# Cosformer attention and a quick-gelu layer on one core: v copied ahead of q's evictions, and three moves in the opening

## The chip, the cores and the metric

The kernel runs on one core of one Trainium2 chip. The metric is the device time of an execution in microseconds. A core has five engines that run side by side and wait for each other through semaphores: PE (TensorE, matrix products, with its weight loads shown as PEld), DVE (VectorE), ACT (ScalarE), POOL (GpSimd) and SP (SyncE). Here POOL and SP issue the transfers between the chip's main memory and the core. PE writes its results into eight banks of an accumulation memory (PSUM), and DVE or ACT carry them from there into the working memory, which the texts call an eviction.

## The reference

Eight batches, eight heads, 576 positions, head size 64, all in float32. The first half is a linear attention with positions weighted by a cosine and a sine; the second half is a layer of 512 to 2048 to 512 with g = h * sigmoid(1.702 h).

```python
def phi(x, c, s):
    r = np.maximum(x, 0.0)
    return np.concatenate([r * c, r * s], axis=-1)
q_p, k_p = phi(q, cos_w, sin_w), phi(k, cos_w, sin_w)
kv = np.einsum('bhsf,bhsd->bhfd', k_p, v)
z = np.sum(k_p, axis=2)
num = np.einsum('bhsf,bhfd->bhsd', q_p, kv)
den = np.einsum('bhsf,bhf->bhs', q_p, z)[..., None] + 1e-06
x = (num / den).transpose(0, 2, 1, 3).reshape(B * S, H * D)
h = x @ w_in
out = (h * (1.0 / (1.0 + np.exp(-1.702 * h)))) @ w_out
```

## The kernel before, in words

The work goes batch by batch. For one batch, q and k are made positive and weighted by the cosine and the sine (`trig`, line 143 on DVE and POOL, line 141 on ACT). The key-value sums `kv_mm` (line 228) multiply the weighted k with v, 72 small matmuls for four pairs of heads. The weighted q is turned so that features lie on partitions. For batches 0 and 1 PE does that with transposes: `qturn_pe` (line 184) fills a PSUM tile with two of the nine slots of 64 positions, and `qevac` evicts it to `qT` on DVE (line 202) or on ACT (line 200). `num_mm` (line 258) makes numerators and denominators of a chunk of 128 positions, `num_div` (lines 264, 266, 308) divides on DVE, `xturn_mm` (line 328) turns the quotient on PE and `xturn_evac` (line 334) evicts it to `xT` on ACT. Then the layer: `mm1` (line 349) makes h for 16 groups of 128 hidden features, `gelu` (line 354, ACT) makes g of each, and `mm2` (line 386) multiplies by w_out for four chunks of 128 rows, in portions of four hidden groups each. Output goes through ACT (line 390) and a transfer that POOL issues (line 394).

Nothing reorders the work: each engine runs its instructions in the order in which the program writes them, and waits come from data and from buffers. So the order of the calls is the schedule. Buffers are few. The eight PSUM banks are four banks m0 to m3, taken in the order 2, 0, 3, 1 or named by `at`, and two tiles of two banks each that `pair` gives in turn. `at_homes` takes such a pair as the home of two `qturn_pe`. In block 0, `ha` holds slots 0 to 3 of batch 1, `hb` slots 4 to 7, and the next pair, which `kv_open` takes for batch 1's key-value sums, is the one that `ha` had: `kv_mm` can't start until both evictions of `ha` are done. Likewise `hc`, for the ninth slot, is the one that `hb` had.

The opening, batch 0, is written out by hand in lines 410 to 490, with its own small steps. `idle` (line 400) gives PE 512-column matmuls on zeros: three in float32 at the start, and one at line 424 and one at line 436, in bfloat16. v of batch 0 comes in bfloat16 straight from memory (`vb`, line 133, in two halves). `den_early` (line 273) and `num1_mm` (line 284) make denominators and numerators of chunks 0 and 1, `num1_div` (line 289) divides, `x1turn_mm` (line 296) turns and `x1turn_evac` (line 300) evicts to `xT`. Slots 6 and 7 of q go one by one through `qslot_pe` (line 189) and `qslot_evac` (line 193), slot 8 through `qturn_pe(4, at=1)`. The first four hidden groups are made chunk by chunk with `part(c, fc)`, matmuls of 128 columns, and the group that follows (`mm1(0, 4)`) takes the bank that the first gelu frees.

Block 0 (lines 500 to 558) is the layer of batch 0 with the attention of batch 1 among its matmuls. k, q and v of batch 1 come in float32 by transfers from POOL's queue (line 116), between the four parts of w_out. `vcopy` brings v of batch 1 into the bfloat16 tile `vt`, for two pairs of heads at a time (line 164 on DVE, line 162 on ACT). From batch 1 on, blocks look alike: `mm1` and `gelu` for 16 groups, then `mm2` with the next batch's key-value sums and numerators between, and q turned by transfers.

Of the kernel before, what the change touches and what calls it, by code (L numbers as in the profile page):

```python
# [19 lines left out]
def kernel(  # L20
# [97 lines left out]
    def load_q(b, eng=nc.sync):  # L118
        eng.dma_start(out=qf[:, 0:2048].rearrange("p (h e) -> p h e", h=H),
                            in_=q[b, :, 0:512, :].rearrange("h (p c) d -> p h (c d)", c=4))  # L120
        eng.dma_start(out=qf[0:64, 2048:2560].rearrange("p (h e) -> p h e", h=H),
                            in_=q[b, :, 512:S, :].rearrange("h p d -> p h d"))

    def load_win(g):
        nc.gpsimd.dma_start(out=w_in_sb[g], in_=win_r[:, :, ts(g, 512)])
# [10 lines left out]
    def trig(dst, src, j, act=False, eng=nc.vector):  # L136
        i = src[:, :, ts(j, 64)]
        for cs, w in enumerate((cosw, sinw)):
            o = dst[:, j, :, ts(cs, 64)]
            if act:  # L140
                nc.scalar.activation(o, i, AF.Relu, scale=w[:, j:j + 1])  # L141
            else:
                eng.tensor_scalar(o, i, 0.0, w[:, j:j + 1], op0=MAX, op1=MUL)  # L143
# [14 lines left out]
    def vcopy(i0, i1, act=False):  # L158
        o = vt[:, :, i0:i1, 0:64].rearrange("p j i e -> p i j e")
        i = vf[:, i0:i1].rearrange("p i (j e) -> p i j e", e=64)  # L160
        if act:
            nc.scalar.activation(o, i, AF.Copy)
        else:
            nc.vector.tensor_copy(o, i)
# [3 lines left out]
    def bank(shape, dt=F32, at=None):  # L168
        if at is None:
            at = (2, 0, 3, 1)[ring["m"] % 4]  # L170
            ring["m"] += 1
        return pmm.tile(shape, dt, name="mm", tag=f"m{at}", bufs=1)
# [7 lines left out]
    def qturn_pe(c, home=None, at=None):  # L180
        tps[c] = bank([128, 2, NI, 128], BF16, at) if home is None else home
        for j in range(2 * c, min(2 * c + 2, NS)):
            for i in range(NI):
                nc.tensor.transpose(tps[c][:, j % 2, i], qn0[:, j, i, :], ident)  # L184
# [10 lines left out]
    def qevac(c, act=False):  # L195
        n = min(2 * c + 2, NS) - 2 * c
        o = qT[:, :, ds(c * 128, n * 64)].rearrange("f h (j p) -> f j h p", j=n)
        i = tps.pop(c)[:, 0:n].rearrange("f j i (hh p) -> f j (i hh) p", hh=2)
        if act:
            nc.scalar.activation(o, i, AF.Copy)  # L200
        else:
            nc.vector.tensor_copy(o, i)  # L202
# [51 lines left out]
    def num_mm(c):  # L254
        ps = pair()
        for h in range(H):
            i, hh = divmod(h, 2)
            nc.tensor.matmul(ps[:, h // 4, ds((h % 4) * 65, 65)], qT[:, h, ts(c, 128)],  # L258
                             st["kvs"][:, hh, i, 0:65], start=True, stop=True)
        nums[c] = [ps]  # L260

    def inv_of(d):
        den = small.tile([128, 2, 4], F32, name="den")
        nc.vector.tensor_scalar(den, d, 1e-6, None, op0=ADD)  # L264
        inv = small.tile([128, 2, 4], F32, name="inv")
        nc.vector.reciprocal(inv, den)
        return inv
# [25 lines left out]
    def x1turn_mm(c):  # L293
        xv = nums.pop(c).rearrange("p a h e -> p (a h e)")
        for kc in range(KC):
            nc.tensor.transpose(st["n", c][:, ts(kc, 64)].bitcast(BF16), xv[:, ts(kc, 128)], ident)  # L296

    def x1turn_evac(b, c):
        i = st["n", c][:, 0:256].bitcast(BF16).rearrange("p (k t) -> p k t", k=KC)
        nc.scalar.activation(x_of(b, c), i, AF.Copy)  # L300

    def num_div(c, inv=None):
        ps = nums[c][0]
        pv = ps[:, :, 0:260].rearrange("p a (h e) -> p a h e", h=4)
        if inv is None:
            inv = inv_of(pv[:, :, :, 64])
        xn = small.tile([128, 2, 4, 64], BF16, name="xn", bufs=4)
        nc.vector.tensor_tensor(xn, pv[:, :, :, 0:64],  # L308
                                inv.unsqueeze(3).to_broadcast([128, 2, 4, 64]), op=MUL)
        nums[c].append(xn)  # L310
# [6 lines left out]
    def x_open(b):  # L317
        x[b] = xpool.tile([128, KC, MT], BF16, name="xT")
# [11 lines left out]
    def xturn_evac(b, c):  # L330
        ps = nums.pop(c)[0]
        i = ps[:, :, 264:392].bitcast(BF16).rearrange("p a (k t) -> p a k t", k=2)
        o = x_of(b, c).rearrange("p (a k) t -> p a k t", a=2)
        nc.scalar.activation(o, i, AF.Copy)

    def xturn_dma(b, c):
        xn = nums.pop(c)[1]
        n = 128 if c < 4 else 64
        nc.sync.dma_start_transpose(out=x_of(b, c), in_=xn[0:n].rearrange("p a h e -> p (a h e)"))
# [5 lines left out]
    def mm1_part(b, fc, t0, t1):  # L345
        if t0 == 0:
            hp[fc] = bank([128, MT])
        for kc in range(KC):
            nc.tensor.matmul(hp[fc][:, t0:t1], w_in_of(kc, fc), x[b][:, kc, t0:t1],  # L349
                             start=(kc == 0), stop=(kc == KC - 1))  # L350
# [30 lines left out]
    def mm2(b, t, lo, hi, c0=0, c1=d_model):  # L381
        if lo == 0:
            yp[t, c0] = bank([128, d_model])
        for fc in range(lo, hi):
            w = gT[fc][:, ts(t, 128)] if t < 4 else gl_t[:, fc, ts(t - 4, 128)]
            nc.tensor.matmul(yp[t, c0][:, c0:c1], w, w_out_sb[:, fc, c0:c1],  # L386
                             start=(fc == 0), stop=(fc == FC - 1))
        if hi == FC:
            ysb = ypool.tile([128, d_model], F32, name="ysb")
            nc.scalar.activation(ysb[:, c0:c1], yp[t, c0][:, c0:c1], AF.Identity)  # L390
            for p0, n, dst in rows(b, t):
                last = b == B - 1 and t != 4 and (t, p0) != (5, 0)
                eng = nc.sync if last else nc.gpsimd
                eng.dma_start(out=dst[:, c0:c1], in_=ysb[p0:p0 + n, c0:c1])  # L394

    def idle(n, w=None, t=warm):
        if w is None:
            w = bank([128, 512], at=0)
        for _ in range(n):
            nc.tensor.matmul(w, t[:, 0:128], t[:, 0:128].unsqueeze(1).to_broadcast([128, 4, 128]),  # L400
                             start=True, stop=True)
        return w
# [7 lines left out]
    w = idle(3, t=warm32)  # L410
# [10 lines left out]
        ksum(j, j == order[0], j == order[-1])  # L421
    for j in (0, 1):
        trig(qn0, qf0, j)
    idle(1, w)
    qturn_pe(0, at=2)
    for j in (2, 3):
        trig(qn0, qf0, j, act=True)
# [5 lines left out]
    nc.gpsimd.tensor_copy(gate[0:1, 1:2], vb[0:1, 3, 0:1])  # L433
    load_win(2)
    load_win(3)
    idle(1, w)
    qturn_pe(1, at=3)
    kv_mm(0, 2, vb_rhs, 0, 64)
    for j in (6, 7):
# [18 lines left out]
    qslot_evac(7)  # L458
    num_mm(2)
    num_div(2)  # L460
    x_open(0)
    x1turn_mm(0)
    x1turn_evac(0, 0)
    qturn_pe(4, at=1)
    num_mm(3)
    num_div(3)
    x1turn_mm(1)
# [3 lines left out]
    def part(c, *fcs):  # L471
        for fc in fcs:
            mm1_part(0, fc, c * 128, c * 128 + 128)
# [6 lines left out]
    part(1, 3)  # L480
    xturn_mm(3)
    xturn_evac(0, 3)
    part(2, 0, 1, 2, 3)
    num_mm(4)
    num_div(4)
    xturn_dma(0, 4)
    part(3, 0, 1, 2, 3)
    for fc in range(4):
        gelu(fc)
    mm1(0, 4)  # L490
# [22 lines left out]
    ha = at_homes()  # L513
    qturn_pe(0, ha[0])
    qturn_pe(1, ha[1])
    qevac(0)
    qevac(1, act=True)
    vcopy(0, 2)
    vcopy(2, 4)
    mm2(0, 3, 4, 8)  # L520
    hb = at_homes()
    qturn_pe(2, hb[0])
    qturn_pe(3, hb[1])
    qevac(2, act=True)
    qevac(3, act=True)
    load_q(2, nc.gpsimd)
    load(kf, k, 2, nc.gpsimd)
    load(vf, v, 2, nc.gpsimd)
# [109 lines left out]
```

## Time and profile before

| | |
|---|---|
| median of 3 runs | 291.74 us (291.6 to 292.91) |
| the profiled execution | 291.65 us |
| its span, first to last instruction | 289.9 us |
| instructions | 5634 |
| granted clock of PE, mean | 0.999 |
| opening, up to the first 512-column matmul of the layer | 20.39 us |
| block 0's last matmul gives way to block 1 | 50.59 us |

A row of the chain of work gives start, length and the work that the end of the program goes back to; "issue" is time in which nothing that the profile shows was waited for. A row of a timeline gives start, length, engine, line, operation, what is written and read, and in brackets the idle time of the engine ahead of it and what ended it. Consecutive instructions of one kind stand in one row with their count; its length runs from the first's start to the last's end. A matmul's length holds its passage through the array, so one of 512 columns shows 0.38 us while the next starts 0.216 us after it; pieces of the chain join such ends. A row of a tile or a line gives the least, median and greatest duration in ns, and for transfers the time from issue to landing.

### The profile page before, as it was taken

How to read it: one execution, taken by the hardware profiler on the slowest of the kernel's cores; microseconds unless marked ns; L12 is line 12 of the kernel's file. 1: busy time of each engine (PE TensorE's matmuls, PEld its weight loads, DVE VectorE, ACT ScalarE, POOL GpSimd, SP SyncE). 2: the span in 40 equal slices, each digit the busy share in tenths (PEclk: the TensorE clock that was granted, in tenths of full speed). 3: DMA queues.
4: the chain of work that ended last, by engine and by line, in shares of the span. 5: the costliest groups of instructions: out<-in, count | busy, mean ns of one | idle time of the engine just before them, and what ended most of it. 6: DMA issues, size and time to landing. Idle time of an engine off the chain costs nothing.

```text
span 289.9 us, 5634 instructions
## 1 busy us (share of the span) xinstructions
PE 285.1 (98%) x2253; PEld 152.8 (53%) x2253; DVE 122.9 (42%) x353; ACT 134.0 (46%) x235; POOL 37.7 (13%) x72
## 2 busy tenths in 40 slices
PE   8999999999999999999999999999999999999995
PEld 3685475555555545555455545554555455554444
DVE  4853566903657364636482567256534200000000
ACT  7977565692157114630463136412651167651111
POOL 6560043201210011001100110011000100002000
PEclk9999999999999999999999999999999999999999
DMA  7999999991999868956896469946962400002322
GB/s 254 240 215 286 372 257 371 233 234 34 134 296 247 192 139 298 260 171 144 256 296 184 129 188 321 232 103 180 324 125 73 119 37 0 0 2 46 85 86 72
DMA packets 67769, 52.46 MB, mean 181 GB/s; under 512 B 47968, under 2 KB 57952, under 8 KB 67744
## 3 DMA queue, kind: packets, MB, share of 16 engines
q1 hardware_dynamic: 60320, 32.52, 44.9%
q0 software_dynamic: 7424, 19.60, 23.9%
q8 instruction: 17, 0.28, 0.4%
q14 instruction: 8, 0.07, 0.1%
HBM read 36.70 MB, written 9.44 MB: 159 GB/s over the span
## 4 chain that ended last, share of the span: by engine, by line
PE 95%; DMA 2%; ACT 2%; DVE 1%; issue 0%; SPq 0%; ACTq 0%; DVEq 0%
PE mm L386 43%; PE mm L349 38%; PE mm L366 5%; PE at L228 3%; PE at L258 3%; DMA kf<-in_k_dram 2%; ACT kr L141 1%; PE mm L184 1%; PE at L328 0%; PE at L184 0%; ACT qT L200 0%; DVE qT L202 0%; DVE xn L289 0%; PE mm L296 0%; ACT xT L300 0%
## 5 line engine op out<-in xcount | busy, mean ns | idle before, releaser
L386 PE MATMUL mm<-w_out_sb,g 128*128 128x512 bf16 (+1 forms) x528 | 118.2, 373 | 0.0
L349 PE MATMUL mm<-xT,w_in 128*128 128x512 bf16 (+1 forms) x560 | 112.7, 361 | 0.1
L354 ACT ACTIVATE g<-mm 128x512 bf16<-128x512 f32 x128 | 75.6, 598 | 31.3 <-PE mm L349 31.3
L349 PEld LDWEIGHTS <-w_in 128*128 128x128 bf16 x560 | 60.0, 113 | 51.2 <-issue 0.2
L386 PEld LDWEIGHTS <-g 128*128 128x128 bf16 x528 | 48.6, 98 | 49.1
L390 ACT ACTIVATE ysb<-mm 128x512 f32<-128x512 f32 (+1 forms) x37 | 21.7, 586 | 105.9 <-PE mm L386 103.0
L394 POOL DMA_DIRECT2D out_dram<-ysb x39 | 21.1, 542 | 205.0 <-ACT ysb L390 204.6
L143 DVE TENSOR_SCALAR kr<-kf,cosw 128x256 bf16<-128x256 f32 x64 | 22.4, 350 | 29.9 <-DMA kf<-in_k_dram 29.9
L308 DVE TENSOR_TENSOR xn<-at,inv 128x512 bf16<-128x512 f32 x38 | 26.3, 691 | 1.3
L143 DVE TENSOR_SCALAR kr<-kf,sinw 128x256 bf16<-128x256 f32 x64 | 22.5, 352 | 0.0
L264 DVE TENSOR_SCALAR den<-at 128x8 f32<-128x8 f32 x38 | 6.3, 166 | 32.9 <-PE at L258 32.9
L233 DVE CAST kvs<-at 128x520 bf16<-128x520 f32 (+1 forms) x9 | 5.8, 640 | 32.9 <-PE at L228 32.9
L258 PEld LDWEIGHTS <-qT 128*128 128x128 bf16 x304 | 14.1, 97 | 8.0
L258 PE MATMUL at<-kvs,qT 128*128 128x65 bf16 x304 | 15.4, 193 | 0.0
L156 DVE TENSOR_SCALAR qn<-qf,sinw 128x512 bf16<-128x512 f32 (+1 forms) x30 | 14.4, 480 | 0.0
L156 DVE TENSOR_SCALAR qn<-qf,cosw 128x512 bf16<-128x512 f32 (+1 forms) x30 | 14.3, 476 | 0.0
L366 PE MATMUL mm<-xt,w_in 128*128 128x512 bf16 x64 | 14.0, 379 | 0.0
L386 PE MATMUL mm<-w_out_sb,gl_t 128*128 128x512 bf16 x64 | 14.0, 379 | 0.0
L367 ACT ACTIVATE gl_t<-mm 128x512 bf16<-128x512 f32 x16 | 9.6, 597 | 4.2 <-PE mm L366 4.2
L228 PEld LDWEIGHTS <-kr 64*128 64x128 bf16 x576 | 9.4, 94 | 2.9 <-issue 2.5
L366 PEld LDWEIGHTS <-w_in 128*128 128x128 bf16 x64 | 7.2, 113 | 6.6
L386 PEld LDWEIGHTS <-gl_t 128*128 128x128 bf16 x64 | 6.2, 98 | 7.5
(78 smaller groups left out, 117.3 us busy)
## 6 DMA issues: line engine op xcount, KB each, us to landing
kf<-in_k_dram SPq DMA_DIRECT2D x5, 1152.0 KB, 6.6
vf<-in_v_dram SPq DMA_DIRECT2D x5, 1152.0 KB, 9.6
qf<-in_q_dram SPq DMA_DIRECT2D x5, 1024.0 KB, 5.5
out_dram<-ysb POOLq DMA_DIRECT2D x20, 256.0 KB, 2.7
out_dram<-ysb POOLq DMA_DIRECT2D x19, 128.0 KB, 3.7
kf<-in_k_dram POOLq DMA_DIRECT2D x2, 1152.0 KB, 10.8
vf<-in_v_dram POOLq DMA_DIRECT2D x2, 1152.0 KB, 15.8
w_in<-in_moe_w_in_dram POOLq DMA_DIRECT2D x4, 512.0 KB, 9.3
```

The source lines that it names most:

```text
L143: eng.tensor_scalar(o, i, 0.0, w[:, j:j + 1], op0=MAX, op1=MUL)
L156: nc.vector.tensor_scalar(o, i, 0.0, sc, op0=MAX, op1=MUL)
L228: nc.tensor.matmul(st["kv", i][:, hh, ds(col, n)], kr[r, j, i, :], rhs(r, i, j), start=(j == 0), stop=(j == NS - 1))
L258: nc.tensor.matmul(ps[:, h // 4, ds((h % 4) * 65, 65)], qT[:, h, ts(c, 128)], st["kvs"][:, hh, i, 0:65], start=True, stop=True)
L308: nc.vector.tensor_tensor(xn, pv[:, :, :, 0:64], inv.unsqueeze(3).to_broadcast([128, 2, 4, 64]), op=MUL)
L349: nc.tensor.matmul(hp[fc][:, t0:t1], w_in_of(kc, fc), x[b][:, kc, t0:t1], start=(kc == 0), stop=(kc == KC - 1))
L354: nc.scalar.activation(g, hp.pop(fc), AF.Gelu_apprx_sigmoid)
L366: nc.tensor.matmul(hps, w_in_of(kc, fc), xt[:, kc, :], start=(kc == 0), stop=(kc == KC - 1))
L367: nc.scalar.activation(gl_t[:, fc, :], hps, AF.Gelu_apprx_sigmoid)
L386: nc.tensor.matmul(yp[t, c0][:, c0:c1], w, w_out_sb[:, fc, c0:c1], start=(fc == 0), stop=(fc == FC - 1))
L390: nc.scalar.activation(ysb[:, c0:c1], yp[t, c0][:, c0:c1], AF.Identity)
L394: eng.dma_start(out=dst[:, c0:c1], in_=ysb[p0:p0 + n, c0:c1])
```

## The change

Four edits. In the opening, the two single idle matmuls are taken out, slot 8's transposes go ahead of the opening of chunk 0's x, and group 0 of the last full chunk goes ahead of chunk 2's group 3, behind the fifth chunk's numerators. In block 0, the two copies of v of batch 1 go ahead of the evictions of `ha`, the second of them on ACT; both evictions of `ha` are on DVE; of `hb`, slots 6 and 7 are evicted first and on DVE, slots 4 and 5 behind them on ACT.

```diff
@@ opening
     for j in (0, 1):
         trig(qn0, qf0, j)
-    idle(1, w)
     qturn_pe(0, at=2)
...
     load_win(3)
-    idle(1, w)
     qturn_pe(1, at=3)
     kv_mm(0, 2, vb_rhs, 0, 64)
...
     num_mm(2)
     num_div(2)
+    qturn_pe(4, at=1)
     x_open(0)
     x1turn_mm(0)
     x1turn_evac(0, 0)
-    qturn_pe(4, at=1)
     num_mm(3)
...
-    part(2, 0, 1, 2, 3)
+    part(2, 0, 1, 2)
     num_mm(4)
     num_div(4)
     xturn_dma(0, 4)
-    part(3, 0, 1, 2, 3)
+    part(3, 0)
+    part(2, 3)
+    part(3, 1, 2, 3)
     for fc in range(4):
         gelu(fc)
@@ block 0
     qturn_pe(0, ha[0])
     qturn_pe(1, ha[1])
+    vcopy(0, 2)
+    vcopy(2, 4, act=True)
     qevac(0)
-    qevac(1, act=True)
-    vcopy(0, 2)
-    vcopy(2, 4)
+    qevac(1)
     mm2(0, 3, 4, 8)
     hb = at_homes()
     qturn_pe(2, hb[0])
     qturn_pe(3, hb[1])
+    qevac(3)
     qevac(2, act=True)
-    qevac(3, act=True)
     load_q(2, nc.gpsimd)
```

## The prediction

> **What bounds the kernel now.** I read the page first, for whether any engine but the matmul engine counts, then the chain of work in order of time, to see where the matmul engine really waits, and then the timelines around the three places that the edits touch.
>
> ```profile
> PE 285.1 (98%) x2253; PEld 152.8 (53%) x2253; DVE 122.9 (42%) x353; ACT 134.0 (46%) x235; POOL 37.7 (13%) x72
> PEclk9999999999999999999999999999999999999999
> PE 95%; DMA 2%; ACT 2%; DVE 1%; issue 0%; SPq 0%; ACTq 0%; DVEq 0%
> ```
>
> PE is busy for 98% of the span, with a granted clock of nine tenths or more in every slice, and it makes up 95% of the chain. The change removes almost no PE work, so the only thing to win is PE's waiting. The chain shows where that is:
>
> ```profile
> 8.66 0.38 PE mm L238
> ...
> 15.74 0.61 ACT xT L300
> ...
> 16.39 0.38 PE mm L349 x4
> ...
> 20.39 10.52 PE mm L349 x48
> ...
> 37.88 0.70 DVE qT L202
> ...
> 38.61 1.03 ACT qT L200
> ...
> 39.68 1.38 PE at L228 x72
> ...
> 50.59 13.82 PE mm L349 x64
> ```
>
> Three releases by another engine matter: at 16.39, at 20.39, and at 39.68, where batch 1's key-value sums (L228) had to wait for q's evictions on DVE and then ACT. From 50.59 on the chain is PE alone up to the last output: 64 matmuls of 512 columns in 13.82 us, 0.216 us each, and nothing behind it is touched. So the whole question is how much earlier PE reaches 50.59.
>
> **The change, part by part.**
>
> *The two idle matmuls.* Each is one 512-column matmul, 0.22 us of PE.
>
> ```profile
> 9.64 0.38 PE L400 MATMUL mm<-warm 128*128 128x512 bf16 x1
> 10.26 0.23 PEld L184 LDWEIGHTS <-qn 128*128 128x128 bf16 x4 [0.19 <-ACT qn L141]
> 10.64 0.71 PE L228 MATMUL at<-vb,kr 64*128 64x64 bf16 x36
> 12.07 0.71 PE L228 MATMUL at<-vb,kr 64*128 64x64 bf16 x36
> L133 POOL DMA_DIRECT2D vb<-in_v_dram x2: 761/840/919, 4.3 to 5.3; - x2
> DMA to landing us min/median/max: 6.3/6.5/6.8
> ```
>
> They gain nothing, because what follows waits for something else. The transposes behind the second one wait at 10.26 for ACT's q in any case. The two halves of v's bf16 copy are issued at 4.3 and 5.3 and land 6.3 and 6.8 later, at 10.6 and 12.1, exactly where the two groups of L228 begin (10.64 and 12.07). That cover is two transfers; were they earlier, at most 0.44 us could come free, and I take 0. [...]
>
> *q's ninth slot ahead of chunk 0's x.* Four transposes (L184 at 14.85) go ahead of chunk 0's x transposes (L296 at 14.62).
>
> ```profile
> 13.84 1.08 ACT L193 ACTIVATE qT<-mm 128x512 bf16<-128x512 bf16 x2 [0.65 <-PE mm L189]
> 13.87 1.29 DVE L289 TENSOR_TENSOR xn<-mm,inv 128x512 bf16<-128x512 f32 x2
> 14.10 0.41 PE L258 MATMUL at<-kvs,qT 128*128 128x65 bf16 x8
> 14.62 0.23 PEld L296 LDWEIGHTS <-xn 128*128 128x128 bf16 x4 [0.24 <-DVE xn L289]
> 14.85 0.39 PE L184 MATMUL mm<-ident,qn 128*128 128x128 bf16 x4
> 15.05 1.29 ACT L300 ACTIVATE xT<-mm 128x512 bf16<-128x512 bf16 x2
> 15.32 0.39 PE L296 MATMUL mm<-ident,xn 128*128 128x128 bf16 x4
> ```
>
> Four transposes take 14.85 - 14.62 = 0.23 us of PE (0.056 each), eight L258 matmuls 0.24 (15.32 less 15.08). So PE stands from 14.34 to 14.62 waiting for DVE's division. The ninth slot can fill that hole only once its bank is free: the bank holds slot 6, evicted by the first of ACT's two L193, which ends near 14.43. So it runs 14.47 to 14.69, and chunk 0's x transposes begin at 14.69, 0.07 late; ACT's first L300 goes from 15.05 to 15.12. Behind it L258 ends at 15.15, and chunk 1's x transposes wait for the second division (13.87 + 1.29 = 15.16): 15.20 instead of 15.32. They reach ACT 0.42 later, as before (15.32 to 15.74, where the second L300 starts and runs to 15.05 + 1.29 = 16.34): 15.62. ACT can then begin: two L193 take 1.08, so a copy follows the one before it after about 0.5, and the first starts at 15.12. It ends near 16.24, so the matmul at 16.39 comes at 16.29. Gain 0.10 us; bounds -0.07 (if ACT's second copy is set by the first) and +0.23 (the four transposes hidden whole).
>
> *Last chunk's group 0 ahead of chunk 2's group 3.*
>
> ```profile
> 18.38 0.60 ACT L334 ACTIVATE xT<-at 128x512 bf16<-128x512 bf16 x1 [0.74 <-PE at L328]
> 19.31 11.60 PE L349 MATMUL mm<-xT,w_in 128*128 128x128 bf16 x64
> 19.74 2.56 ACT L354 ACTIVATE g<-mm 128x512 bf16<-128x512 f32 x5 [0.77 <-PE mm L349]
> ```
>
> Chunk 3's 16 matmuls begin at 19.31 and at 0.056 are issued by 20.21, but group 4 starts at 20.39: its bank waits for the first gelu, which began at 19.74, 0.43 after 19.31, and takes 0.60. PE waits 0.18. Afterwards four matmuls of chunk 2 (0.22) come behind: chunk 3's group 0 starts at 19.09, its x (ACT 18.38 + 0.60 = 18.98) is there, gelu runs 19.52 to 20.12, while PE is busy until 20.21. The wait goes; gain 0.18. That is the upper bound; the lower is 0, if ACT comes to gelu no sooner than now. The fifth chunk's numerators, division and transposing DMA move up 0.2 with it; that DMA is the only one behind SP's queue there and nobody waits for it. Sum up to here 0.28.
>
> *Block 0: v ahead of q's evictions.* Before: DVE evicts q's first half, ACT the second, then DVE copies both halves of v.
>
> ```profile
> 36.78 0.35 DVE L143 TENSOR_SCALAR qn<-qf,sinw 128x256 bf16<-128x256 f32 x1
> 38.49 1.80 DVE L164 CAST vt<-vf 128x1152 bf16<-128x1152 f32 x2
> L164 DVE CAST vt<-vf x2: 909/942/976, 38.5 to 39.4; 128x1152 bf16<-128x1152 f32 x2
> L116 POOL DMA_DIRECT2D vf<-in_v_dram x1: 830/830/830, 17.1 to 17.1; - x1
> DMA to landing us min/median/max: 18.0/19.1/20.1
> 10.33 1.28 DVE L202 COPY qT<-mm 128x1024 bf16<-128x1024 bf16 x2
> 65.11 1.21 ACT L162 ACTIVATE vt<-vf 128x1152 bf16<-128x1152 f32 x1
> 38.55 1.06 PE L184 MATMUL at<-ident,qn 128*128 128x128 bf16 x16
> 39.99 1.94 ACT L200 ACTIVATE qT<-at 128x1024 bf16<-128x1024 bf16 x2 [0.36 <-ACT qT L200]
> 41.00 1.04 PE L386 MATMUL mm<-w_out_sb,g 128*128 128x512 bf16 x4
> 41.98 0.38 PE L184 MATMUL at<-ident,qn 128*128 128x128 bf16 x4
> 66.06 1.26 PE L228 MATMUL at<-vt,kr 64*128 64x65 bf16 x72
> 67.25 1.90 PE L386 MATMUL mm<-w_out_sb,g 128*128 128x512 bf16 x8
> ```
>
> DVE is done with q at 36.78 + 0.35 = 37.13. The copy needs v, whose load was issued at 17.1 and took the longer 20.1: 37.2. Both fall together, with no margin (before, the copy began at 38.49, 1.3 after the landing). So: copy of v's first half 37.2 to 38.1 (1.80 / 2), then q's two evictions back to back, 1.28 as at 10.33: 39.4. L228 starts at 39.44 instead of 39.68, gain 0.24. PE itself would be there sooner: the 16 transposes at 38.55 are through at 39.45, less 0.28 from the opening is 39.17. So the opening's gain does not add here; DVE's chain takes its place.
>
> ACT's half of v: ACT may be held until DVE's half is done (its q eviction at 38.61 started 0.03 after DVE's ended at 37.88 + 0.70, although the columns differ), so 38.2, plus 1.21: 39.4, or 39.8 with the 0.36 that ACT lost at 39.99. The second half of L228 wants it at 39.44 + 0.60 = 40.04. Hidden. Before, that half came at 38.49 + 1.80 = 40.29 and held L228 up: 41.00 - 39.68 = 1.32 from its start to the next matmul, against 67.25 - 66.06 = 1.19 in block 1. Gain 0.13.
>
> At 41.98 PE waited again: four matmuls from 41.00 take 4 x 0.216 = 0.86, so 0.12 was lost to ACT's last eviction (39.99 + 1.94 = 41.93). Afterwards DVE takes chunk 3 (39.42 to 40.1) and ACT chunk 2 behind it (to about 41.15), and PE comes at 41.50. Gain 0.12. The loads of batch 2 on POOL's queue stand behind the same q work as before and the v load behind the copies, which end sooner: 0.
>
> *Sum.* 0.24 + 0.13 + 0.12 = 0.49 us, all of it visible at 50.59. The profiled execution took 291.65 us (span 289.9), 0.09 under the median 291.74: 291.16 for it, and **291.25 us** for the median, 0.17% less. A difference under 0.5% (1.46 us) is about what a measurement of this kernel cannot tell from none.
>
> [...]
>
> **The rivals.**
>
> *A, the forecast:* 291.25.
>
> *B, v lands late (the slower side).* The copy now stands in front of both evictions on DVE, with q's second copy on ACT, so each 0.1 us by which v lands after 37.2 holds L228 by 0.1. It decides from 0.49 late (37.7): then the time is as before. If it slips by the distance between q's landing and v's (20.1 + 17.1 less 18.0 + 16.3, 2.8 us), the time is 291.25 + 2.8 = 294.1. For it: landing and need coincide, and this transfer took 20 us. Against: nothing ahead of it in its queue is changed.
>
> [...]
>
> *D, DVE's chain is slower than I sum it.* Copy, eviction, eviction with no overlap (0.98, 0.70, 0.70, with 0.04 between, from 37.2) end at 39.7: L228 gains nothing, the 0.25 behind it stays: 291.5.
>
> *E, v lands a little early* or DVE overlaps more, and PE's own 39.17 counts: 0.51 + 0.25 = 0.76 at most: 291.0.
>
> **How the numbers follow.** A 0.60, E 0.10, D 0.14, B 0.10 (0.04 of it beyond half a per cent, that is v over 1.95 us late), C 0.03 (0.01 beyond, if half rate lasts longer), 0.03 for what I have not seen, a third of it faster and a third slower by over half a per cent. Faster by over 0.5% would need 1.46 us, twice all the waits that the three places hold: 0.01. Slower: 0.04 + 0.01 + 0.01 = 0.06. Within: 0.93. Range: E at the low end with 0.1 us for the spread of the runs, 290.9; at the high end D and the mild half of B, 292.1.
>
> **What would show it.** Right: L228's first group still at 10.6 and the second at 12.1 with no idle matmul; the 48 matmuls at 20.39 begin near 20.1; DVE's first copy of v starts within 0.1 of v's landing, two L202 follow it, and L228 starts near 39.45 and takes 1.2; no wait at the ninth slot; the block's last PE piece ends near 50.1. Wrong: DVE idle before the copy for v's DMA, a granted clock under 1.0 before 16, or ACT's half of v ending after 40.0.

## The result, and the profile after

The changed kernel takes 291.01 us (median of 22 runs, 290.84 to 292.25) where the kernel before, run beside it, takes 291.92 (22 runs, 291.58 to 293.56): ratio 0.9966, 95% interval 0.9956 to 0.9976. Run again on another occasion beside further experiments it took 291.22 against 291.81: ratio 0.9974, interval 0.9964 to 0.9984. So it is faster by about 0.3%, 0.6 to 0.9 us, where the prediction said 0.17%, 0.49 us.

The profiled execution of the changed kernel took 292.25 us, longer than that of before (291.65). It has to be read first for why. These are lines of its page:

```profile
PE 282.6 (97%) x2218; PEld 152.4 (52%) x2251; DVE 123.6 (43%) x354; ACT 133.3 (46%) x234; POOL 37.9 (13%) x72
PE 93%; DMA 4%; ACT 2%; issue 1%; ACTq 0%; POOL 0%
```

The chain has 4% of DMA instead of 2%, and PE has lost 2%. The chain in order of time (start, length, what) says which transfer:

```profile
4.27 7.64 DMA vb<-in_v_dram
11.91 0.04 issue
11.95 0.71 PE at L228 x36
...
39.71 0.89 PE at L184 x16
40.61 1.19 PE at L228 x72
```

In this execution the first half of v's bf16 copy landed at 11.91, not 10.60, and PE stood waiting for it. The transfer is issued at 4.3 in both, ahead of everything that the change touches. In the fourteen executions profiled for this study the first L228 starts anywhere from 10.55 to 11.95, each time 0.04 to 0.05 behind this landing, and the earliest of them is a kernel that differs from the changed one in the place of one slot alone. So the late landing is not put down to the change, and executions are compared from the start of the first L228. The rows of PE's timeline for the changed kernel that mark the stages:

```profile
20.27 1.93 PE L349 MATMUL mm<-xT,w_in 128*128 128x128 bf16 x22
40.54 1.26 PE L228 MATMUL at<-vt,kr 64*128 64x65 bf16 x72
41.73 1.04 PE L386 MATMUL mm<-w_out_sb,g 128*128 128x512 bf16 x3
66.69 1.26 PE L228 MATMUL at<-vt,kr 64*128 64x65 bf16 x72
```

The last 20 matmuls of 128 columns start at 20.27 and pass at 0.056 us each (20 take 1.12 us in the chain, at 18.18), so group 4 starts at 21.39. The stages, in us:

| stage of PE | before | changed | difference |
|---|---|---|---|
| first L228 to group 4 (opening) | 9.75 | 9.44 | -0.31 |
| group 4 to batch 1's key-value sums | 19.29 | 19.15 | -0.14 |
| those sums, to the next matmul | 1.32 | 1.19 | -0.13 |
| from there to batch 2's sums (66.06 and 66.69) | 25.06 | 24.96 | -0.10 |
| batch 2's sums to the end of the span | 223.88 | 223.86 | -0.02 |
| all | 279.30 | 278.60 | -0.70 |

### The profile page after: what moved, and what is told of

It reads as the page before. It is cut to its first block, busy times and chain, and to the rows that moved or that the text cites. A ratio compares the mean times of both kernels' runs of the same rounds, so it can differ in the third digit from the quotient of the medians.

```text
span 290.5 us, 5598 instructions
## 1 busy us (share of the span) xinstructions
PE 282.6 (97%) x2218; PEld 152.4 (52%) x2251; DVE 123.6 (43%) x354; ACT 133.3 (46%) x234; POOL 37.9 (13%) x72
## 3 DMA queue, kind: packets, MB, share of 16 engines
HBM read 36.70 MB, written 9.44 MB: 159 GB/s over the span
## 4 chain that ended last, share of the span: by engine, by line
PE 93%; DMA 4%; ACT 2%; issue 1%; ACTq 0%; POOL 0%
PE mm L386 43%; PE mm L349 37%; PE mm L366 5%; PE at L228 3%; PE at L258 3%; DMA vb<-in_v_dram 3%; ACT g L354 1%; DMA kf<-in_k_dram 1%; PE at L184 1%; PE at L328 0%; PE mm L184 0%; ACT xT L300 0%; PE mm L284 0%; PE mm L273 0%; PE mm L189 0%
## 5 line engine op out<-in xcount | busy, mean ns | idle before, releaser
L386 PE MATMUL mm<-w_out_sb,g 128*128 128x512 bf16 (+1 forms) x506 | 116.7, 372 | 1.3 <-issue 0.2
L143 DVE TENSOR_SCALAR kr<-kf,cosw 128x256 bf16<-128x256 f32 x64 | 23.0, 360 | 27.1 <-DMA kf<-in_k_dram 27.1
L228 PEld LDWEIGHTS <-kr 64*128 64x128 bf16 x576 | 9.3, 94 | 3.7 <-issue 3.4
```

The costliest lines, as they stand in the source:

```text
L228: nc.tensor.matmul(st["kv", i][:, hh, ds(col, n)], kr[r, j, i, :], rhs(r, i, j), start=(j == 0), stop=(j == NS - 1))
```

## The experiments

Three theories stood against each other. A: in block 0 PE's own arrival decides, so the opening's gain and block 0's add up. B, the prediction's: DVE's chain behind v's landing decides there and takes the place of the opening's gain. C: the gain is that of the idle matmuls.

For every kernel the table gives the median of its runs, the ratio to the runs of before beside it, and from its profile the start of the first L228, the span, and the span less that start, which leaves the varying landing out. Two profiles each of the changed kernel, and of it with the idle matmuls, agree within 0.04 us in the last but one column, while their spans differ by 0.37 and 0.28 us. The kernel before has one profile. The rows were not all run side by side, so medians of different rows are not compared without their ratios: the runs of before that belong to the rows below the first two have medians of 291.81 to 291.87.

| kernel | median us (runs) | ratio, 95% interval | first L228 | span | rest | to before |
|---|---|---|---|---|---|---|
| before | 291.92 (22) | 1 | 10.64 | 289.94 | 279.30 | 0 |
| changed | 291.01 (22) | 0.9966, 0.9956 to 0.9976 | 11.95 | 290.55 | 278.60 | -0.70 |
| changed, again | 291.22 (8) | 0.9974, 0.9964 to 0.9984 | 11.54 | 290.18 | 278.64 | -0.66 |
| block 0's edit alone | 291.55 (12) | 0.9994, 0.9985 to 1.0004 | 10.77 | 289.62 | 278.85 | -0.45 |
| the opening's edits alone | 291.60 (12) | 0.9993, 0.9984 to 1.0002 | 10.85 | 289.95 | 279.10 | -0.20 |
| idle matmuls out, alone | 291.82 (12) | 0.9999, 0.9988 to 1.0010 | 10.81 | 290.10 | 279.29 | -0.01 |
| changed, idle matmuls back | 291.20 (12) | 0.9984, 0.9972 to 0.9996 | 10.91 | 289.57 | 278.66 | -0.64 |
| the same, again | 291.28 (11) | 0.9978, 0.9967 to 0.9988 | 11.23 | 289.85 | 278.62 | -0.68 |
| changed, ninth slot last | 291.09 (11) | 0.9977, 0.9967 to 0.9987 | 10.55 | 289.21 | 278.66 | -0.64 |
| changed, v late | 293.24 (5) | 1.0047, 1.0034 to 1.0060 | 11.05 | 291.50 | 280.45 | +1.15 |
| before, v late | 292.49 (10) | 1.0018, 1.0004 to 1.0032 | 10.74 | 290.76 | 280.02 | +0.72 |
| before, loads of batch 2 later | 291.86 (10) | 0.9997, 0.9982 to 1.0013 | 10.79 | 290.07 | 279.28 | -0.02 |
| changed, both copies on DVE | 291.62 (10) | 0.9980, 0.9966 to 0.9993 | 10.84 | 289.85 | 279.01 | -0.29 |
| changed, `hb` evicted as before | 291.41 (10) | 0.9981, 0.9968 to 0.9995 | 10.83 | 289.81 | 278.98 | -0.32 |

**Block 0's edit alone.** The kernel before with

```diff
+    vcopy(0, 2)
+    vcopy(2, 4, act=True)
     qevac(0)
-    qevac(1, act=True)
-    vcopy(0, 2)
-    vcopy(2, 4)
+    qevac(1)
...
+    qevac(3)
     qevac(2, act=True)
-    qevac(3, act=True)
```

> Block 0's edit alone, opening as before. Theory A (PE's own arrival decides in block 0, v lands in time): the key-value sums start when PE has turned hb, 0.14 us earlier than in the kernel before, lose no 0.13 in the middle and no 0.12 at the ninth slot: 0.39 us faster than before, 0.3 us slower than the changed kernel. Theory B (DVE's chain behind v's landing decides, as the prediction had it): the start hangs on DVE at 39.44 and not on PE, so the opening's gain is swallowed and this kernel is as fast as the whole change, 0.39 to 0.49 us faster than before. Theory C (the gain comes from the idle matmuls, block 0 gives nothing that lasts): as before.

**The opening's edits alone.** The other three edits, block 0 as before.

> The three edits of the opening alone (no idle matmuls, ninth slot and group 0 moved), block 0 as before. Theory A: 0.3 us faster than before, all of it carried through block 0's waits, because there DVE waited for PE's transposes. Theory B: the same 0.28. Theory C: 0.5 us or more faster, and fewer long executions than the kernel before has.

Measured from the first L228, block 0's edit alone gives 0.45 and the opening's alone 0.20, together 0.65, and the whole change 0.66 to 0.70. These parts rest on one profile each. By the runs alone neither part stands clear of no change (the intervals reach 1.0004 and 1.0002). Block 0 alone is 0.2 slower than the whole in the profiles, where theory B had it as fast, and the chain of work shows why. In this kernel it goes through block 0 without DVE:

```profile
38.79 0.89 PE at L184 x16
39.68 1.19 PE at L228 x72
```

Before, DVE's and ACT's evictions stood in the chain ahead of L228. Now PE comes from its transposes straight to the sums. So theory B falls: the opening's gain is not swallowed by the change in block 0. Theory A's 0.39 and 0.3 are right in sum and off by 0.06 and 0.1 in the parts. Where the opening's 0.1 went is in DVE's and PE's timelines of that kernel:

```profile
37.80 0.69 DVE L202 COPY qT<-at 128x1024 bf16<-128x1024 bf16 x1 [0.54 <-PE at L184]
38.41 2.02 DVE L164 CAST vt<-vf 128x1152 bf16<-128x1152 f32 x2
39.66 1.54 PE L228 MATMUL at<-vt,kr 64*128 64x65 bf16 x72
```

PE comes earlier, but with the old order the two copies of v stand behind q's eviction and take 2.02 us here (1.80 in the profile of before). The sums start at 39.66, when the first copy is done, and take 1.48 to the next matmul instead of 1.32: 0.16 is lost there, and 0.11 comes back at the ninth slot, where PE no longer waits (42.01 - 41.14 = 0.87 for four matmuls). So it is the old order in block 0 that swallowed part of the opening's gain, not the new one.

**The idle matmuls.** Taken out alone, and put back into the changed kernel.

```diff
-    idle(1, w)
     qturn_pe(0, at=2)
...
-    idle(1, w)
     qturn_pe(1, at=3)
```

> Only the two single idle matmuls removed. Theory A and B: no difference (under 0.1 us), since v's two halves release the two groups of key-value sums. Theory C: 0.2 to 0.45 us faster, the idle matmuls' own time on PE. If the clock needs them: a granted clock under 1.0 ahead of 16 us and 1 us slower.

> The changed kernel with the two idle matmuls put back. Theory A and B: as the changed kernel, 0.7 to 0.9 us faster than before. Theory C: 0.2 to 0.45 us slower than the changed kernel.

> The changed kernel with the two idle matmuls, now beside the changed kernel on the same chip. If the idle matmuls cost nothing (theory A) the two agree within 0.1 us. If they do bear on the time once block 0 no longer waits (theory C in part): 0.15 to 0.25 us slower than the changed kernel.

> The changed kernel once more, beside the others on one chip. Theory A: 0.65 to 0.75 us faster than before (0.3 of the opening, 0.4 of block 0). Theory B would have given 0.49 and is out if this is above 0.6.

Alone they give 0.01 us from the first L228 on. That column starts behind the idle matmuls, so it can't show what they cost ahead of it. For that there is the landing: with and without them the first L228 starts 0.04 to 0.05 behind it (11.23 behind 11.18 with them, 11.54 behind 11.50 without, in the changed kernel). In the runs beside each other the medians are 291.22 without and 291.28 with them in the changed kernel, 291.84 with and 291.82 without them in the kernel before, and the rest of the span is the same, 278.64 and 278.62. Theory C falls. On theory B, which was to be out above 0.6, the changed kernel's second comparison gave 0.66 by the profile but 0.59 by the medians: the runs alone do not put it out. The granted share of the clock is 1.00 from 8 to 14 us with them, in the profile of before, and it is 1.00 there without them too, in the execution where v's half landed latest. Here are three windows of the changed kernel's profile (the stretch and its length, then busy time and count of PE, PEld, DVE, ACT and POOL, then the granted share of the clock, the DMA share and GB/s) and two rows of PE's timeline:

```profile
8.00:10.00 2.00, 1.46 (x8) 0.39 (x6) 1.49 (x6) 1.82 (x5) 0.00 (x0) 1.00 1.17 273
10.00:12.00 2.00, 1.00 (x16) 0.81 (x18) 1.48 (x5) 2.00 (x6) 0.27 (x2) 1.00 1.22 207
12.00:14.00 2.00, 2.00 (x85) 1.77 (x85) 1.36 (x4) 1.16 (x3) 2.00 (x2) 1.00 1.23 206
9.49 1.48 PE L184 MATMUL mm<-ident,qn 128*128 128x128 bf16 x16 [0.43 <-DVE qn L143]
11.95 0.71 PE L228 MATMUL at<-vb,kr 64*128 64x64 bf16 x36 [0.98 <-DMA vb<-in_v_dram]
```

From the end of the last L238 at 9.07 to 11.95 PE does 16 transposes and waits: 2.9 us, and the granted share stays 1.00 through all three windows.

**Ninth slot last.** The changed kernel with slot 8 behind chunk 1's x.

```diff
     num_div(2)
-    qturn_pe(4, at=1)
     x_open(0)
...
     x1turn_evac(0, 1)
+    qturn_pe(4, at=1)
     qevac(4, act=True)
```

> The changed kernel, but the ninth slot's transposes stand behind chunk 1's x transposes. In the changed kernel PE waits 0.32 us there for ACT's copy of chunk 0's x, which starts 0.05 late because of the slot ahead of it. Theory A: chunk 0's x comes 0.05 to 0.07 earlier, the third group of matmuls behind it 0.03 to 0.07 earlier: as the changed kernel or up to 0.07 us faster. If instead the place ahead of chunk 0's x is what gives the gain: 0.1 us slower than the changed kernel.

No difference: 278.66 against 278.60 and 278.64. Both places take the slot out of the way of chunk 1's x, and which of the two it gets does not show. It is no version that beats the changed kernel.

**v late.** The load of v changes places with the third part of w_out on POOL's queue, in the changed kernel and in the kernel before.

```diff
-    load(vf, v, 1)
     load_wout(2)
+    load(vf, v, 1)
```

> The changed kernel with v's load one place later in POOL's queue, behind the third part of w_out, so that v lands near 39.7 instead of 37.3. Rival B's mechanism (every 0.1 us of later landing holds the key-value sums by 0.1, since q's evictions stand behind the copy on DVE): the sums start near 41.8, 2.2 to 2.4 us slower than the changed kernel, 293.2 to 293.5. If the evictions could pass or PE's work covered it: under 1 us slower.

> The kernel before with v's load one place later, as in the changed kernel with late v. There the evictions stand ahead of the copy and are done by 39.6; the sums wait for the copies alone: first copy 39.5 to 40.4, second to 41.2. 0.8 to 1.0 us slower than before, against 1.85 to 2.0 us by which the same landing slows the changed kernel. If the order on DVE doesn't matter: 1.9 us slower too.

DVE's and PE's timelines of the changed kernel with late v:

```profile
39.48 0.76 DVE L164 CAST vt<-vf 128x1152 bf16<-128x1152 f32 x1 [2.50 <-DMA vf<-in_v_dram]
40.16 1.88 DVE L202 COPY qT<-at 128x1024 bf16<-128x1024 bf16 x3
41.49 1.26 PE L228 MATMUL at<-vt,kr 64*128 64x65 bf16 x72 [1.76 <-DVE qT L202]
```

v landed 2.1 us later (39.46 for 37.33) and DVE waited for it with both evictions behind it, so PE's sums waited too: 280.45 against 278.60 and 278.64, 1.8 us, where 2.2 to 2.4 was expected. The mechanism of rival B is real, at its price less 0.3 of slack. The kernel before loses 0.72 from about the same landing:

```profile
39.60 1.62 DVE L164 CAST vt<-vf 128x1152 bf16<-128x1152 f32 x2 [0.94 <-DMA vf<-in_v_dram]
40.42 1.57 PE L228 MATMUL at<-vt,kr 64*128 64x65 bf16 x72 [0.73 <-DVE vt L164]
```

There both evictions of `ha` are done by 39.71 and the sums wait for the copies alone. So the new order has made the kernel depend on one landing for which it has little to spare: 0.2 us where the opening is early (first L228 at 10.55 and 10.91), more where it is late.

**Loads of batch 2 later.** In the kernel before, with POOL held until the sums are evicted:

```diff
-    load_q(2, nc.gpsimd)
-    load(kf, k, 2, nc.gpsimd)
-    load(vf, v, 2, nc.gpsimd)
     kv_open()
     kv_mm(0, 4, vt_rhs, 0, 65)
     kv_evac(0, 4)
+    nc.gpsimd.tensor_copy(gate[0:1, 2:3], st['kvs'][0:1, 0, 0, 0:1])
+    load_q(2, nc.gpsimd)
+    load(kf, k, 2, nc.gpsimd)
+    load(vf, v, 2, nc.gpsimd)
     mm2(0, 0, 8, 12)
```

> The kernel before, with POOL's loads of batch 2 held back until batch 1's key-value sums are evicted, so that POOL issues nothing while DVE copies v. In the kernel before DVE's copies of v took 0.91 to 0.98 us with POOL issuing beside them; in the changed kernel the copy took 0.76 ahead of POOL's first issue. Theory P (POOL's issuing slows DVE's copy): both copies take 0.76, the wait in the middle of the key-value sums goes, 0.1 us faster than before. Rival Q (the copy is slowed by ACT's eviction or by PE at work beside it, which are still there): copies of 0.9 us or more and no gain.

Its timelines of DVE, PE and ACT:

```profile
38.63 1.42 DVE L164 CAST vt<-vf 128x1152 bf16<-128x1152 f32 x2
39.82 1.26 PE L228 MATMUL at<-vt,kr 64*128 64x65 bf16 x72
40.14 1.94 ACT L200 ACTIVATE qT<-at 128x1024 bf16<-128x1024 bf16 x2 [0.38 <-ACT qT L200]
41.01 1.04 PE L386 MATMUL mm<-w_out_sb,g 128*128 128x512 bf16 x4
42.13 0.38 PE L184 MATMUL at<-ident,qn 128*128 128x128 bf16 x4
```

Theory P's durations are right: without POOL's issues two copies take 1.42 and not 1.80, and the wait in the middle of the sums is gone (41.01 - 39.82 = 1.19). But nothing is gained: 279.28. The next wait takes it back. ACT's last eviction ends at 42.08, 31.29 behind the first L228 as in the kernel before (41.93 - 10.64), and the ninth slot starts at 42.13, where four matmuls from 41.01 would have been through at 41.87: a wait of 0.26 instead of 0.12.

**Both copies on DVE.** The changed kernel with `vcopy(2, 4)` instead of `vcopy(2, 4, act=True)`.

> The changed kernel with both copies of v on DVE ahead of q's evictions (no half on ACT). DVE's chain is then 37.3 + 0.76 + 0.8 to 1.2 (POOL issues beside the second) + 1.28: the sums start at 40.2 to 40.6 instead of 39.3 to 39.6, 0.8 to 1.2 us slower than the changed kernel and slower than before by 0.2 to 0.5. If PE's own arrival decides in any case: as the changed kernel.

DVE, PE and POOL:

```profile
37.16 1.43 DVE L164 CAST vt<-vf 128x1152 bf16<-128x1152 f32 x2
39.84 1.26 PE L228 MATMUL at<-vt,kr 64*128 64x65 bf16 x72 [0.36 <-DVE qT L202]
37.96 1.10 POOL L119 DMA_DIRECT2D qf<-in_q_dram  x1 [16.56 <-ACT qn L141]
```

Slower than the changed kernel by 0.4 (279.01 against 278.60 and 278.64), less than the 0.8 to 1.2 expected: DVE's second copy was not slowed, it took as long as the first, and it was POOL's issue that took 1.10 us instead of 0.91. The half on ACT is worth 0.4 us. In this kernel DVE's chain behind v's landing does decide, as the prediction had it for the changed one.

**`hb` evicted as before.** The changed kernel with slots 4 to 7 evicted by ACT, chunk 2 first.

> The changed kernel, but slots 4 to 7 evicted as before, both by ACT, chunk 2 first. Prediction's step: the wait of 0.12 at the ninth slot comes from ACT's second eviction ending late; it returns here, 0.1 us slower than the changed kernel. Rival: ACT is free sooner now (its half of v ends at 38.9, where it evicted q till 39.6 before), both evictions end before PE needs the buffer and nothing is lost.

```profile
40.61 1.04 PE L386 MATMUL mm<-w_out_sb,g 128*128 128x512 bf16 x4
41.86 0.38 PE L184 MATMUL at<-ident,qn 128*128 128x128 bf16 x4 [0.22 <-ACT qT L200]
39.87 1.94 ACT L200 ACTIVATE qT<-at 128x1024 bf16<-128x1024 bf16 x2 [0.98 <-PE at L184]
```

It is 0.32 to 0.38 slower than the four profiles of the changed kernel with and without the idle matmuls, where 0.1 was expected. ACT was free, but PE has turned the slots only at 39.48, ACT starts 0.4 later, and two evictions on one engine end at 41.81; PE would have been at the ninth slot at 40.61 + 0.86 = 41.47. With the sums earlier, this wait would have grown from 0.12 to 0.39. The division between DVE and ACT is worth about 0.35 here, three times what the prediction gave for it. Why ACT starts 0.4 behind PE's transposes, where DVE starts 0.1 behind them (40.71 for 40.61 in the changed kernel), the trace does not show.

## Why the prediction was right or wrong

*What bounds the kernel.* Right. Behind batch 2's sums the two profiles differ by 0.02 us. All that the change gives it gives ahead of 51 us.

*The idle matmuls, 0.* Right, and for the reason given: v's two transfers release both groups of L228, also in the changed kernel's late profile (landings at 11.91 and 13.30, groups at 11.95 and 13.34). In the profile of the changed kernel PE waits for the first even 0.98 us. The chances hold 0.03 for C, a clock at half rate without the idle matmuls. No run shows a half rate: in the changed kernel's profile the granted share is 1.00 in every window from 8 to 16 us, over the 2.9 us in which PE has no matmul but transposes, and the mean granted clocks of its 22 runs are 0.998 to 1.0. A longer stretch no run here shows.

*The opening, 0.28.* Right, in size and step: from the first L228 to group 4 it is 9.44 and 9.47 in the two profiles of the changed kernel against 9.75, 0.28 to 0.31 less. The parts come out as well: from the second L228 to chunk 1's matmuls it is 4.68 and 4.67 against 4.76 (12.07 to 16.83), about 0.09 where 0.10 was said for the ninth slot, and the other 0.19 comes at the last chunk, where 0.18 was said. Chunk 0's x is 0.04 later (17.05 - 11.95 = 5.10 against 15.70 - 10.64 = 5.06), as was worked out with 0.07, and no wait for gelu stands ahead of group 4.

*Block 0's start, 0.24.* Here the prediction went wrong, in the sentence that the opening's gain does not add and DVE's chain takes its place. The term that was mis-sized is the copy of v on DVE. These are DVE, ACT and POOL in the changed kernel:

```profile
37.35 0.76 DVE L164 CAST vt<-vf 128x1152 bf16<-128x1152 f32 x1
37.77 1.15 ACT L162 ACTIVATE vt<-vf 128x1152 bf16<-128x1152 f32 x1
38.89 1.29 DVE L202 COPY qT<-at 128x1024 bf16<-128x1024 bf16 x2 [0.78 <-PE at L184]
38.16 0.91 POOL L119 DMA_DIRECT2D qf<-in_q_dram  x1 [16.36 <-DVE vt L164]
```

I gave the copy 0.90, from a stretch in which POOL issued transfers beside it. Ahead of POOL's first issue it takes 0.76. With the late opening, here, DVE even waits 0.78 for PE. These are DVE and PE with an earlier one, where DVE's chain is tightest (the changed kernel with the idle matmuls, first L228 at 10.91):

```profile
37.40 0.76 DVE L164 CAST vt<-vf 128x1152 bf16<-128x1152 f32 x1
38.08 1.28 DVE L202 COPY qT<-at 128x1024 bf16<-128x1024 bf16 x2
38.58 1.06 PE L184 MATMUL at<-ident,qn 128*128 128x128 bf16 x16
39.57 1.26 PE L228 MATMUL at<-vt,kr 64*128 64x65 bf16 x72
```

The first eviction starts 0.68 behind the copy's start, not 0.90, and both evictions end at 39.36, 1.96 behind that start where 2.2 was summed. The sums start at 39.57, when PE is through with its transposes. The chain of work, too, goes from PE's transposes to the sums in this profile and in all the others of the changed kernel, also with slot 8 last. So PE decides, as rival E had it, and the opening's gain goes through. Rival E, with 291.0, had a chance of 0.10. Its bound of 0.76 was worked out without the change from transposes to sums on PE, about 0.1 (39.57 - 38.58 = 0.99, where 16 transposes take 0.90).

*ACT's half of v.* I let ACT wait for DVE's half; it does not (37.77 against 38.11). It was hidden either way.

*The middle of the sums, 0.13, and the ninth slot, 0.12.* 0.13 and 0.10 by the stages. But the two hang together: with the middle alone removed, in the late loads, the wait at the ninth slot grew to 0.26, and with the start and the middle removed, in the `hb` run, to 0.39. The start removed alone no run shows.

*The sum.* 0.49 predicted; by profile 0.66 to 0.70, in the runs 0.91 and 0.59. With PE's own arrival in the place of DVE's chain the steps give 0.28 for the opening, 0.14 at the start of the sums (the 0.23 that PE stood there, less 0.09 for the change from transposes to sums), 0.13 and 0.12: 0.67. That the forecast time of 291.25 lies near both medians, 291.01 and 291.22, is partly luck: it left out the opening's 0.28 and had 0.10 too much at the start of the sums. The first comparison's 0.91 is more than the profiles explain; ten of the 22 runs of before there took 292.0 us or more, one of the changed kernel. A late landing of v's first half could do that (it cost 1.3 us in the profile of the changed kernel), but those runs have no trace, and it stays open.

*Rival B* did not come: in all profiles where the load kept its place in the queue v landed between 36.96 and 37.41. But its mechanism was shown. (Its distance between q's landing and v's is 2.9 by its own figures, not 2.8; nothing else hangs on that.) *Rival D* is out: copy and two evictions took less than I summed, not more.

## What to carry to other kernels

When a chain of several engines ends in one wait, removing its links one by one can give nothing: the wait moves to the next link, as with the 0.13 in the middle of the sums, which removed alone left 279.28 for 279.30. Work out who would be last after all edits together, and take each duration from a stretch in which the same engines will be at work beside it, not from where the operation stands now: here the copy took 0.76 where 0.90 was summed. Compare executions from the first event that every later one hangs on, if its landing varies more than the effect sought (here 1.4 us for an effect of 0.7), and judge what lies ahead of that event by other means.

## What the runs showed that was not expected

DVE's copy of 128x1152 from float32 to bfloat16 took 0.75 to 0.76 us where POOL issued nothing (0.76 at 37.35 in the changed kernel, ahead of POOL's issue at 38.16) and 0.90 to 1.19 where POOL issued transfers at the time (0.91 and 0.98 in the kernel before, with issues at 38.00 and 38.90). Or it kept its 0.76, and it was POOL's issue that took longer: 1.10 instead of 0.91 with both copies on DVE, 1.08 and 1.09 instead of 0.77 to 0.87 in the two kernels with late v. With late v POOL's issue starts 0.02 and 0.03 ahead of DVE's copy in the records. Why it is the copy that takes longer in one kernel and the issue in another, no run shows.

The start of the first L228, set by a landing, varied by 1.4 us among fourteen executions, while the distance from there to the end repeated within 0.04 us for each of the two programs that were profiled twice. The time around the span was 1.70 to 1.74 us in twelve profiles and 1.96 and 1.86 in two (block 0's edit alone, and the later loads), which lies outside what the trace shows.
